# Loads and stores that ScalarE's queue may issue beside SyncE's, in a planned attention and FFN kernel on one Trainium2 core

## The chip, the core and the metric

The kernel runs on one core of one Trainium2 chip. A core has TensorE for matrix products (PE in the profile, with its weight loads on a row of their own, PEld), VectorE (DVE), ScalarE (ACT), GpSimd (POOL) and SyncE (SP), which here does nothing but issue transfers (DMAs). Each engine works through its instructions in the order of the program and starts one when the semaphores it waits for have been set. A transfer is issued on an engine's queue, which takes that engine some time, and is then carried out by the core's 16 DMA engines. The metric is the device time of one execution in microseconds (us).

## The reference

Causal attention over 8 batches, 8 heads, 576 positions and head size 64, with a bias from a cumulated sum, then a two-layer network with an ELU between its layers (4608 rows, 512 to 2048 to 512). All in float32:

```python
scores = scale * np.matmul(q, k.transpose(0, 1, 3, 2))          # scale = 1 / 8
cum = np.cumsum(np.maximum(s, 0.0), axis=-1)
bias = -(cum[:, :, :, None] - cum[:, :, None, :])
scores = np.where(causal, -1000000000.0, scores + np.minimum(bias, 0.0))
attn = softmax(scores)
x = rows_of(np.matmul(attn, v))                                 # 4608 x 512
h = x @ w_in
g = np.where(h > 0.0, h, np.exp(np.minimum(h, 0.0)) - 1.0)
return g @ w_out
```

## The kernel before

**Tiles and stages.** The attention works on pairs of heads, 32 of them (8 batches, 4 pairs). For each pair `prepare_pair` (L1018) loads the keys of both heads (`stk`) and the queries (`stq`; six transfers a pair at most), takes their largest values on ScalarE (the lines with `junk` as output, L699 and L702), scales and splits each into two 16-bit halves (`parts`), writes these to DRAM (`spread<-parts`) and reads them back in the layout of the products (`set<-spread`). `softmax_block` (L1130) computes for one block of 128 query rows the score products (`sc`, L1141), mask and row minimum on VectorE (`mn`, L1144) and the exponential on ScalarE (`p`, L1149). The first 64 rows of both heads are a small block of their own, with `None` at the end of its names (`tr_None`, `psh_None`). `halved` (L1170) writes the normalized rows as two 16-bit halves, and `turned_load` (L479) has a transposing DMA (`T<-p`, DMA_TRANSPOSE) turn them, 4 to 17 units of 128 x 128 at a time, because `weighing` (L1279) needs them turned for its products with the values (`av`, L1328). The values come by batch in `group_values` (L973, `va`), with their own largest values (L702) and halves (`v`). The attention's rows go to DRAM (`x_dram<-x`) and come back as columns (`xc<-x_dram`).

The network runs over 18 chunks of 256 rows, `moe_chunk` (L1457): first layer `h` (L1499, L1503: three products of 16-bit halves of x and w_in), ELU in steps on ScalarE and VectorE (`g` L1515, L1522 or L1526, `h` L1535, `gg` L1539 and L1542), second layer `o` (L1560), the output copy `ost` (L1586) and its store `out_dram<-ost` (L1612). Chunks and attention pairs are mixed so that TensorE has products of the one while the other is being prepared. The two weights are loaded (`raws`) and split at the start, until about 204 us.

**What sets the order.** No loop of the code is the order of the program. Every operation is recorded as an `Op` with its reads and writes and one or more *ways*: an engine, a cost in ns that the code assumes, the function that emits it, and for a transfer also its bytes and the time it is taken to be under way. `run` (L249) then places one operation after another: of all that may come next, the way that would be finished first on its engine, and of the operations the one that could start earliest; among those of that engine that could start as early, the one with the least deadline (`late`) goes first. `issue` (L234) makes eight trial runs; after each, `deadlines` (L211) goes back through the order and gives each operation the time by which it must start for the run to end as it did. The deadlines of the best trial give the order that is emitted. So a number such as `SP_COST` is no duration on the chip: it decides which order is built.

All 863 transfers of the program are issued by SyncE: `load` (L475) and `turned_load` offer only that way. SyncE's assumed cost is 500 ns for a load, 640 for those of keys and queries, and for a transposing DMA 170 ns a unit but at least 1330.

At the start TensorE gets *fillers* (L1618 to L1623: transposes of the identity into `scratch`, whose result nobody reads) wherever the plan has nothing else for it, until 60 us of the plan's time. They are ops too, and up to 300 of them may be placed.

## Time and profile before

| | us |
|---|---|
| median of 3 runs (lowest, highest) | 1020.22 (1017.01, 1020.98) |
| profiled execution, device time | 1021.47 |
| profiled execution, span | 1019.7 |
| mean granted clock of TensorE | 0.998 |

The span is the time from the first to the last instruction; the device time of the same execution is 1.8 us more. The busy tenths of the engines in 40 equal slices, with the share of the DMA engines:

```profile
PE   8999999999989999999999999999999999999998
DVE  6899899989989898999998998898979898744343
ACT  5999776776667676676776777666657665533232
DMA  7888743688999997899889999989979998521000
```

Each digit is a share in tenths, 9 standing for 90% or more. What an engine is called busy with leaves out the issuing of transfers. The same profile's chain, followed back from the last instruction, and its costliest groups of instructions (line, engine, operation, output<-inputs, count, busy us, mean ns of one, idle us just before them and what ended most of it):

```profile
PE h L1503 19%; PE o L1560 19%; PE sc L1141 3%; PE av L1328 3%; DMA T<-p 1%; DVE p L1209 1%; DVE p L1144 1%; DMA stq<-in_qT_dram 0%; DVE gg L1542 0%; DVE h L1535 0%; DMA spread<-parts 0%; ACT p L1149 0%; DVE p L1203 0%; DVE parts L1064 0%; ACT g L1522 0%
...
L1503 PE MATMUL h<-xh,wp 128*128 128x256 f16 x2176 | 401.5, 273 | 0.0
L1560 PE MATMUL o<-wp,gg 128*128 128x512 f16 x1632 | 391.2, 379 | 4.1 <-DVE tops L723 1.5
L1503 PEld LDWEIGHTS <-wp 128*128 128x128 f16 x3264 | 317.4, 98 | 66.1 <-issue 1.3
L1503 PE MATMUL h<-xl,wp 128*128 128x256 f16 x1088 | 296.9, 273 | 0.0
```

### The profile page before, as it was taken

Reading aid. Unit: us, or ns where it says so; the run is one execution under the profiler, and the core shown is the slowest. Engines: PE = TensorE matmul, PEld = TensorE weight load, DVE = VectorE, ACT = ScalarE, POOL = GpSimd, SP = SyncE. Lnnn points to the kernel's source line nnn. Section 1 sums busy time; section 2 is a strip of 40 time slices with the busy share of each in tenths; the row PEclk is TensorE's granted clock in tenths of the full one; section 3 lists DMA queues with packets and bytes.
Section 4 is the critical chain, followed back from the end, with each engine's and each line's share of the span. In section 5 each row is a group of like instructions: output and inputs, shape, how many; then the busy total and the mean of one; then the engine's idle time right before and its main releaser. Section 6 shows DMA issues by size and latency. Waiting matters only on the chain.

```text
span 1019.7 us, 21777 instructions
## 1 busy us (share of the span) xinstructions
PE 997.2 (98%) x7327; PEld 686.5 (67%) x7327; DVE 846.5 (83%) x2352; ACT 660.1 (65%) x1583; POOL 261.1 (26%) x429
## 2 busy tenths in 40 slices
PE   8999999999989999999999999999999999999998
PEld 7677666666656666666666666666766666666665
DVE  6899899989989898999998998898979898744343
ACT  5999776776667676676776777666657665533232
POOL 6332272423232323322222222221412330100000
PEclk9999999999999999999999999999999999999999
DMA  7888743688999997899889999989979998521000
GB/s 205 251 256 274 208 130 87 133 224 162 195 205 205 225 224 178 191 223 214 184 181 225 199 185 203 239 185 240 189 177 217 204 210 180 92 69 43 1 22 21
DMA packets 296724, 179.83 MB, mean 176 GB/s; under 512 B 209908, under 2 KB 270564, under 8 KB 296612
## 3 DMA queue, kind: packets, MB, share of 16 engines
q1 hardware_dynamic: 296612, 178.45, 76.6%
q8 instruction: 57, 0.93, 0.4%
q14 instruction: 55, 0.45, 0.1%
HBM read 93.08 MB, written 36.81 MB: 127 GB/s over the span
## 4 chain that ended last, share of the span: by engine, by line
PE 45%; DVE 4%; DMA 2%; issue 1%; ACT 1%; SPq 0%; DVEq 0%; ACTq 0%
PE h L1503 19%; PE o L1560 19%; PE sc L1141 3%; PE av L1328 3%; DMA T<-p 1%; DVE p L1209 1%; DVE p L1144 1%; DMA stq<-in_qT_dram 0%; DVE gg L1542 0%; DVE h L1535 0%; DMA spread<-parts 0%; ACT p L1149 0%; DVE p L1203 0%; DVE parts L1064 0%; ACT g L1522 0%
## 5 line engine op out<-in xcount | busy, mean ns | idle before, releaser
L1503 PE MATMUL h<-xh,wp 128*128 128x256 f16 x2176 | 401.5, 273 | 0.0
L1560 PE MATMUL o<-wp,gg 128*128 128x512 f16 x1632 | 391.2, 379 | 4.1 <-DVE tops L723 1.5
L1503 PEld LDWEIGHTS <-wp 128*128 128x128 f16 x3264 | 317.4, 98 | 66.1 <-issue 1.3
L1503 PE MATMUL h<-xl,wp 128*128 128x256 f16 x1088 | 296.9, 273 | 0.0
L1560 PEld LDWEIGHTS <-gg 128*128 128x128 f16 x1632 | 156.8, 98 | 152.8 <-DVE gg L1542 5.9
L1149 ACT ACTIVATE p<-p,mn 128x192 f32<-128x192 f32 (+1 forms) x232 | 144.0, 621 | 80.1 <-DVE mn L1144 77.5
L1209 DVE SCALAR_TENSOR_TENSOR p<-p,sm,p 128x512 f16<-128x512 f32 (+3 forms) x258 | 155.1, 630 | 3.4 <-ACT p L1205 1.5
L1515 ACT ACTIVATE g<-h,cs 128x512 f32<-128x512 f32 x136 | 92.4, 679 | 77.1 <-PE h L1503 75.5
L1539 ACT ACTIVATE gg<-h 128x512 f16<-128x512 f32 x127 | 75.4, 593 | 85.5 <-DVE h L1535 84.7
L1542 DVE SCALAR_TENSOR_TENSOR gg<-h,gg 128x512 f16<-128x512 f32 x136 | 93.2, 685 | 25.0 <-ACT gg L1539 24.5
L1141 PE MATMUL sc<-set 128*128 128x288 f16 (+3 forms) x544 | 109.7, 298 | 2.9 <-DVE mn L1144 1.6
L1144 DVE CUSTOM_DVE_ANT_0 p<-sc,maskw 128x192 f32<-128x192 f32 (+1 forms) x232 | 108.6, 480 | 4.2 <-PE sc L1141 1.8
L1535 DVE SCALAR_TENSOR_TENSOR h<-g,cs,h 128x512 f32<-128x512 f32 x136 | 101.9, 749 | 9.1 <-ACT g L1522 5.2
L1201 POOL TENSOR_SCALAR p<-p,sm 128x512 f16<-128x512 f32 (+3 forms) x78 | 53.6, 691 | 217.6 <-DVE sm L1155 80.3
L1205 ACT ACTIVATE p<-p,sm 128x512 f16<-128x512 f32 (+3 forms) x152 | 79.1, 532 | 26.5 <-ACT p L1149 8.3
L1526 DVE TENSOR_SCALAR g<-g 128x512 f32<-128x512 f32 x81 | 36.3, 448 | 58.1 <-ACT g L1515 57.7
L1141 PEld LDWEIGHTS <-set 128*128 128x128 f16 x584 | 55.1, 98 | 35.8 <-issue 6.0
L1328 PEld LDWEIGHTS <-v 128*64 128x64 f16 x960 | 48.5, 111 | 24.4 <-issue 13.7
L1328 PE MATMUL av<-T,v 128*64 128x256 f16 (+5 forms) x960 | 62.3, 281 | 2.1 <-DMA T<-p 2.0
L500 POOL TENSOR_SCALAR v<-va,scales 128x320 f16<-128x320 f32 (+1 forms) x41 | 25.3, 620 | 98.7 <-PE av L1328 66.8
L500 POOL TENSOR_SCALAR xh<-xc,cs 128x512 f16<-128x512 f32 x22 | 16.7, 760 | 130.0 <-PE h L1503 127.0
L1149 ACT ACTIVATION_READ_ACCUMULATOR p<-p,mn 128x1 f32 x232 | 43.6, 188 | 0.0
(205 smaller groups left out, 1271.2 us busy)
## 6 DMA issues: line engine op xcount, KB each, us to landing
set<-spread SPq DMA_DIRECT2D x32, 432.0 KB
spread<-parts_None SPq DMA_DIRECT2D x32, 288.0 KB
set<-spread SPq DMA_DIRECT2D x32, 288.0 KB
raws<-in_w_in_dram SPq DMA_DIRECT2D x16, 512.0 KB
raws<-in_w_out_dram SPq DMA_DIRECT2D x16, 512.0 KB
out_dram<-ost SPq DMA_DIRECT2D x32, 256.0 KB
va<-in_vb_dram SPq DMA_DIRECT2D x16, 352.0 KB
xc<-x_dram SPq DMA_DIRECT2D x22, 256.0 KB
```

Source lines behind the costliest of these rows:

```text
L1141: pe_.matmul(view(sc.v[:, :cw]), l, r, start=n == 0, stop=n == len(pairs) - 1)
L1144: op(prio, [("DVE", 168 + cw + 55 * (i > 0), lambda i=i, sc=sc: dve.tensor_tensor_reduce(pt.v[:, i * cw : (i + 1) * cw], sc.v[:, :cw], mv( ...
L1149: op(prio, [("ACT", 383 + w / 1.2, lambda: act.activation(pt.v[:, :w], pt.v[:, :w], AF.Exp, bias=mn.v[:, n - 1 : n], scale=-1.0, accum_out ...
L1205: ("ACT", 295 + size / 1.2, lambda part=part: act.activation(part(0), own(part), AF.Copy, scale=sm.v[:, r])),
L1209: ("DVE-SB", dve_2(size), lambda part=part: dve.scalar_tensor_tensor(part(1), own(part), sm.v[:, r], part(0), ALU.mult, ALU.subtract)),
L1328: pe_.matmul(av.v[w.h * HB : (w.h + 1) * HB, dst], w.values.v[:, w.h, kb, v], part(w, kb, m), start=kb == 0 and m == 0 and v == 0, stop=kb ...
L1503: pe_.matmul(columns(k), weight_part(f, 0, part)[1]()[:, c * P : (c + 1) * P], xx.v[:, c], start=(c == 0 and m == 0), stop=(c == NCB - 1 a ...
L1515: op(side, [("ACT", act_c(W) + (0 if native else 90), lambda: act.activation(g.v, hp.v, AF.Exp, scale=1.0 if native else by(3)))], [hp] + ...
L1535: op(side, [("DVE", dve_p(W) + 60, lambda: dve.scalar_tensor_tensor(hp.v, g.v, by(2 if sign[0] else 1), hp.v, ALU.mult, ALU.max))], [g, cs ...
L1539: ("ACT", act_c(W), lambda: act.activation(gg.v[:, 0], hp.v, AF.Copy, scale=2.0**-DOWN)),
L1542: op(side, [("DVE", dve_p(W), lambda: dve.scalar_tensor_tensor(gg.v[:, 1], hp.v, 2.0**-DOWN, gg.v[:, 0], ALU.mult, ALU.subtract))], [hp, ( ...
L1560: pe_.matmul(acc[i].v, gg.v[:, g, at], weight_part(f, 1, part)[1](), start=(f == 0 and m == 0), stop=(f == NF - 1 and m == 2),)
```

## The change

`load` can be given `either=True`; then the plan has two ways for that transfer, SyncE's queue and ScalarE's, with 600 ns assumed for an issue on ScalarE. This is set for the loads of values, keys and queries and for the stores of the result. The assumed costs of SyncE's own issues rise (500 to 520, 170 to 195 a unit, at least 1440 for a transposing DMA). In `deadlines` a filler no longer sets a deadline for what stands before it. The trial runs go from eight to six. The deadline by which the order is sorted is kept apart from the one being worked out (`due` and `late`).

```diff
--- before.py
+++ after.py
@@ -43,7 +43,8 @@
 
 N_CUT, CUT, N_LOW = 4, 2, 3
 PRIO_LOW = 10
-SP_COST, SP_SHORT, SP_TURN = 500.0, 640.0, 170.0
+SP_COST, SP_SHORT, SP_TURN = 520.0, 640.0, 195.0
+ACT_COST = 600.0
 
 N_FREE = 0
 
@@ -92,7 +93,7 @@
 
 
 class Op:
-    __slots__ = ("ways", "after", "before", "behind", "bufs", "new", "prio", "ready", "left", "filler", "late", "at", "frees")
+    __slots__ = ("ways", "after", "before", "behind", "bufs", "new", "prio", "ready", "left", "filler", "late", "at", "due")
 
 
 class Plan:
@@ -186,7 +187,7 @@
             d.before.append(o)
         for d in firsts:
             d.behind.append(o)
-        o.left, o.ready, o.late = len(o.after) + len(firsts), {}, 0.0
+        o.left, o.ready, o.due = len(o.after) + len(firsts), {}, 0.0
         self.ops.append(o)
         return o
 
@@ -215,21 +216,21 @@
             engine, start, stop, lag = o.at
             t = late.get(engine, end)
             for d in o.before:
-                if d.at is not None:
+                if d.at is not None and not d.filler:
                     t = min(t, d.late - lag - self.HOPS.get((engine, d.at[0]), self.HOP))
             for b in o.bufs:
                 for d in b.followed:
                     t = min(t, d.late - lag - self.HOPS.get((engine, d.at[0]), self.HOP))
             t -= stop - start
             for d in o.behind:
-                if d.at is not None:
+                if d.at is not None and not d.filler:
                     t = min(t, d.late)
             o.late = t
             if engine in late:
                 late[engine] = t
 
     ENDS = ("PE",)
-    ROUNDS, WAIT = 8, {"PE": 0.0, "DVE": 0.0, "ACT": 0.0, "Pool": 0.0, "SP": 0.0}
+    ROUNDS, WAIT = 6, {"PE": 0.0, "DVE": 0.0, "ACT": 0.0, "Pool": 0.0, "SP": 0.0}
 
     def issue(self):
         best = None
@@ -238,11 +239,13 @@
             self.wait = n > 0
             end, order = self.run(False)
             if best is None or end < best[0]:
-                best = end, self.wait, [(o, o.late) for o in self.ops]
+                best = end, self.wait, [(o, o.due) for o in self.ops]
             self.deadlines(order, end)
+            for o in order:
+                o.due = o.late
         _, self.wait, lates = best
-        for o, late in lates:
-            o.late = late
+        for o, due in lates:
+            o.due = due
         self.reset()
         return self.run(True)
 
@@ -317,7 +320,7 @@
             until, engine = first[0] + (self.WAIT[first[2]] if self.wait else 0.0), first[2]
             start, _, _, n, o = min(
                 (x for x in found if x[2] == engine and (x[0] <= until and not x[4].filler or x is first)),
-                key=lambda x: (x[4].late, x[1]))
+                key=lambda x: (x[4].due, x[1]))
             if o.filler:
                 start -= GAP
             engine, cost, trace = o.ways[n][:3]
@@ -472,13 +475,14 @@
     op = plan.op
     act, dve, pool, pe_ = nc.scalar, nc.vector, nc.gpsimd, nc.tensor
 
-    def load(prio, dst, src, reads, writes, nbytes, late=(), lag=LAG, cost=SP_COST):
-        return op(prio, [("SP", cost, lambda: nc.sync.dma_start(dst(), src()), lag, nbytes)],
-                  reads, writes, late)
+    def load(prio, dst, src, reads, writes, nbytes, late=(), lag=LAG, cost=SP_COST, either=False):
+        ways = [("SP", cost, lambda: nc.sync.dma_start(dst(), src()), lag, nbytes),
+                ("ACT", ACT_COST, lambda: act.dma_start(dst(), src()), lag, nbytes)]
+        return op(prio, ways[: 1 + either], reads, writes, late)
 
     def turned_load(prio, units, dst, src, reads, writes):
 
-        op(prio, [("SP", max(1330.0, SP_TURN * units), lambda: nc.sync.dma_start_transpose(dst(), src()), LAG,
+        op(prio, [("SP", max(1440.0, SP_TURN * units), lambda: nc.sync.dma_start_transpose(dst(), src()), LAG,
                    units * P * P * 2.2)], reads, writes)
 
     def rounded(prio, n, dst, src, reads, writes, sign=1.0, only=None):
@@ -981,10 +985,10 @@
         va = plan.buf(sb, [P, NP, nv, D], F32, f"va_{at}", tag=home.key[1])
         for j in range(NP):
             load(prio + j, lambda j=j: va.v[:, j, :whole], lambda j=j: vb[u.b, j, :, s0 : s0 + whole], [],
-                 [(va, (j, "whole"))], P * whole * D * 4)
+                 [(va, (j, "whole"))], P * whole * D * 4, either=True)
             for rows in HALF[: nv - whole]:
                 load(prio + j, lambda j=j, rows=rows: va.v[rows, j, whole:], lambda j=j: vb[u.b, j, :HB, s0 + whole : s0 + nv],
-                     [], [(va, (j, rows.start))], HB * 2 * D * 4)
+                     [], [(va, (j, rows.start))], HB * 2 * D * 4, either=True)
             peak(prio, nv * D, lambda j=j: va.v[:, j], values_of(va, j), first + j, mybir.AxisListType.XY,
                  aside=lambda: unread(nv * D).rearrange("p (n d) -> p n d", d=D))
         scales_of(prio, [(first, NP + 1)], col)
@@ -1026,15 +1030,15 @@
         spread = spreads[pair_sets.index(o)]
         for m, rows in enumerate(HALF):
             load(prio, lambda m=m, rows=rows: sk.v[rows, :n], lambda m=m: kT[b, :HB, 2 * j + m, :n], [], [(sk, m)],
-                 HB * n * 4, cost=SP_SHORT)
+                 HB * n * 4, cost=SP_SHORT, either=True)
         for m, rows in enumerate(HALF):
             if c0:
                 at = (1 - m) * (w - HB)
                 load(prio, lambda rows=rows, at=at: sq.v[rows, at : at + HB],
-                     lambda m=m: qT[b, j, :HB, m * HB : (m + 1) * HB], [], [(sq, (m, 0))], HB * HB * 4, cost=SP_SHORT)
+                     lambda m=m: qT[b, j, :HB, m * HB : (m + 1) * HB], [], [(sq, (m, 0))], HB * HB * 4, cost=SP_SHORT, either=True)
             load(prio, lambda m=m, rows=rows: sq.v[rows, m * c0 : m * c0 + nb * P].rearrange("d (i t) -> d i t", t=P),
                  lambda m=m: qT[b, j, :HB, P:].rearrange("d (i m t) -> d i m t", m=2, t=P)[
-                     :, u.blocks[0] : u.last + 1, m], [], [(sq, (m, 1))], HB * P * nb * 4, cost=SP_SHORT)
+                     :, u.blocks[0] : u.last + 1, m], [], [(sq, (m, 1))], HB * P * nb * 4, cost=SP_SHORT, either=True)
         peak(prio, w, lambda: sq.v[:, :w], [sq], 0, aside=lambda: unread(w), dst=pk)
         peak(prio, n, lambda: sk.v[:, :n], [sk], 1, aside=lambda: unread(n), dst=pk)
 
@@ -1611,7 +1615,7 @@
                     r0 = b * S + r + lo - t
                     load(side, lambda r0=r0, n=up - lo: out[r0 : r0 + n, :],
                          lambda ost=ost, o=slice(lo - i * P, up - i * P): ost.v[o],
-                         [ost], [], (up - lo) * DM * 4)
+                         [ost], [], (up - lo) * DM * 4, either=True)
                 t += n
         return following
```

In the program built after the change, 176 of the 863 transfers are on ScalarE: 54 of 72 loads of keys, 75 of 112 of queries, 26 of 44 of values and 21 of 40 stores. Since the order of all engines comes out of the plan, it is another one from the start. Three places, each with the rows of the program as it stands in the queue (line, operation, output<-input, shape, and xN for N such rows in sequence; the number at a name's end is the tile's own, and lines after the change are 1 to 4 higher).

SyncE before, at its start, from the loads of the first pairs to the first piece of the weights (`kl` are keys, `vs` and `va` values, `raws` weights):

```order
L476 DMA vs_115<-in_vb_dram 128x448
L476 DMA kl_2_122<-in_kT_dram 64x2x320
L476 DMA vs_133<-in_vb_dram 128x448
L476 DMA va_138<-in_vb_dram 128x320 x4
L476 DMA va_138<-in_vb_dram 64x128 x8
L476 DMA low_queries<-in_qT_dram 64x640
L476 DMA sums_dram<-aux 64x576
L476 DMA kl_1_109<-aux 1x2x320
L476 DMA kl_3_255<-in_kT_dram 64x2x320
L476 DMA raws<-in_w_in_dram 128x4x256
```

SyncE after, the same place:

```order
L479 DMA vs_121<-in_vb_dram 128x448
L479 DMA kl_2_131<-in_kT_dram 64x2x320
L479 DMA vs_141<-in_vb_dram 128x448
L479 DMA va_94<-in_vb_dram 64x128 x3
L479 DMA kl_3_232<-in_kT_dram 64x2x320
L479 DMA sums_dram<-aux 64x576
L479 DMA kl_1_114<-aux 1x2x320
L479 DMA low_queries<-in_qT_dram 64x640
L479 DMA raws<-in_w_in_dram 128x4x256
```

and ScalarE after, the first rows of its program:

```order
L685 ACT_TABLE_LOAD
L685 ACTIVATE junk<-ident 128x1
L480 DMA va_94<-in_vb_dram 128x320 x3
L480 DMA va_94<-in_vb_dram 64x128 x3
L480 DMA va_94<-in_vb_dram 128x320
L480 DMA va_94<-in_vb_dram 64x128 x2
L706 ACTIVATE junk,peaks<-va_94 128x448
```

Nine of the twelve loads of values have gone from SyncE's start to ScalarE's, ahead of ScalarE's first work on them; the first weights stand nine rows nearer to SyncE's start.

SyncE before, where pair 1's queries (`stq_1_None`) are loaded, some 280 us into the profiled execution:

```order
L476 DMA stq_1_None_3778<-in_qT_dram 64x64
L476 DMA stq_1_None_3778<-in_qT_dram 64x4x128
L476 DMA spread_1445<-parts_0_None_3755 256x1x576 x2
L476 DMA stq_1_None_3778<-in_qT_dram 64x4x128
L476 DMA stq_1_None_3778<-in_qT_dram 64x64
L476 DMA stk_2_None_3851<-in_kT_dram 64x576
L481 DMA_TRANSPOSE T_2_0_0_3854<-p_4_2_0_0_0_3813 128x4x128
L481 DMA_TRANSPOSE T_2_0_0_3854<-p_4_2_0_0_0_3813 128x6x128
```

SyncE after, the same queries:

```order
L479 DMA stq_1_None_3443<-in_qT_dram 64x4x128
L479 DMA stq_1_None_3443<-in_qT_dram 64x64
L479 DMA stq_1_None_3443<-in_qT_dram 64x4x128
L479 DMA spread_1499<-parts_0_None_3412 256x1x576 x2
L479 DMA xc_1_3497<-x_dram 128x2x256
L485 DMA_TRANSPOSE T_1_0_0_3524<-p_4_1_0_0_0_3507 128x4x128
```

and ScalarE after, from its one load of these queries to the work that reads them:

```order
L480 DMA stq_1_None_3443<-in_qT_dram 64x64
L1519 ACTIVATE g_1_3451<-h_1_3383,cs_2874 128x512
L1153 ACTIVATE p_161,sm_1_0_0_3356<-p_161,mn_1_0_0_2_3437 128x448
L1526 ACTIVATE g_1_3451<-g_1_3451 128x512
L1153 ACTIVATE p_168,sm_1_0_0_3356<-p_168,mn_1_0_0_3_3449 128x576
L480 DMA stk_2_None_3490<-in_kT_dram 64x576 x2
L1209 ACTIVATE p_4_1_0_0_0_3507<-p_125,sm_1_0_0_3356 128x2x128
```

One of the four loads has gone to ScalarE, between its other work, and both loads of the next pair's keys with it. The three that stayed now stand ahead of an earlier half of the pair's transposes (`T_1_0_0`); the four of `T_2_0_0` come 20 rows behind them.

SyncE before, around two transposes of 17 units, some 790 to 801 us into the execution:

```order
L481 DMA_TRANSPOSE T_1_0_2_11165<-p_2_1_0_2_2_11100 128x17x128
L476 DMA set_1902<-spread_1602 64x2x1152
L476 DMA set_1902<-spread_1602 64x1152
L476 DMA set_1902<-spread_1602 64x3456
L476 DMA set_1902<-aux_dram 3x2x576
L476 DMA xc_1_11244<-x_dram 128x2x256
L476 DMA out_dram<-ost_1_11032 128x512
L476 DMA stk_2_0_2_11257<-in_kT_dram 64x576
L476 DMA x_dram<-x_0_1_2_11251 128x256
L481 DMA_TRANSPOSE T_1_1_2_11282<-p_2_1_1_2_2_11200 128x17x128
```

SyncE after, around the same two:

```order
L485 DMA_TRANSPOSE T_1_0_2_11108<-p_2_1_0_2_2_11009 128x17x128
L479 DMA x_dram<-x_0_1_2_11115 128x256
L479 DMA set_1840<-spread_1654 64x2x1152
L479 DMA set_1840<-spread_1654 64x1152
L479 DMA set_1840<-spread_1654 64x3456
L479 DMA xc_0_11180<-x_dram 128x2x256
L485 DMA_TRANSPOSE T_1_1_2_11203<-p_2_1_1_2_2_11138 128x17x128
```

The store of the result and the keys that stood between the two transposes are no longer there; five issues lie between them where eight did.

## The prediction

> **What bounds the kernel now.** I read the page's head first, then the busy time by stage, then who waited for whom on TensorE and ScalarE, and last the timeline around the longest of those waits.
>
> ```profile
> span 1019.7 us, 21777 instructions
> PE 997.2 (98%) x7327; PEld 686.5 (67%) x7327; DVE 846.5 (83%) x2352; ACT 660.1 (65%) x1583; POOL 261.1 (26%) x429
> ```
>
> TensorE is busy 98% of the span and the change leaves its products alone, so only its gaps can be won: 1019.7 less 997.2 is 22.5 us. The stages say where they lie (stretch in us, its length, busy us of PE, PEld, DVE, ACT, POOL, then clock, share of the DMA engines, GB/s):
>
> ```profile
> 0.00:76.50 76.50, 71.02 (x494) 56.11 (x496) 64.19 (x215) 60.32 (x189) 34.51 (x91) 1.00 0.82 237
> 127.50:204.00 76.50, 74.27 (x501) 50.01 (x500) 74.93 (x194) 55.83 (x134) 37.23 (x46) 1.00 0.48 117
> 204.00:357.00 153.00, 145.58 (x1087) 97.58 (x1086) 136.82 (x394) 104.53 (x258) 45.98 (x69) 1.00 0.95 203
> 357.00:867.00 510.00, 506.63 (x3917) 347.71 (x3916) 456.86 (x1285) 347.35 (x808) 125.83 (x187) 1.00 0.93 202
> 867.00:1020.00 153.00, 148.71 (x1071) 100.14 (x1069) 68.92 (x128) 50.63 (x88) 5.82 (x10) 0.99 0.18 41
> ```
>
> 5.5 us of gap lie in the start, 2.2 in the stretch where the weights are split and VectorE is full (74.9 of 76.5), 4.3 at the end. Between 204 and 867 us, where nearly all the moved transfers are, the gaps are 7.4 + 3.4 = **10.8 us**. VectorE is at 593.7 of 663 there (90%), ScalarE at 451.9 (68%). TensorE's own waits in that stretch (us in total, times, longest):
>
> ```profile
> PE tr_None L1294 <- ACT psh_None L1166: 2.2, 1, 2.2
> PE av L1328 <- DMA T<-p: 2.0, 1, 2.0
> PE sc L1141 <- DVE mn L1144: 1.6, 3, 0.8
> PE sc L1141 <- DVE pc_None L1227: 1.1, 1, 1.1
> PE o L1560 <- DVE gg L1542: 1.0, 3, 0.5
> PE av_None L1287 <- ACT x_None L1340: 1.0, 1, 1.0
> PE o L1560 <- ACT gg L1539: 0.8, 1, 0.8
> ```
>
> The names at their ends are ScalarE and VectorE, but those had been waiting themselves. ScalarE's waits for loads in the same stretch:
>
> ```profile
> ACT junk L702 <- DMA stq_None<-in_qT_dram: 7.8, 6, 2.9
> ACT junk L702 <- DMA va<-in_vb_dram: 6.3, 6, 3.0
> ACT junk L702 <- DMA stq<-in_qT_dram: 5.2, 6, 1.8
> ```
>
> That is 19.3 us of ScalarE standing before a load of queries or values. The longest, on SyncE's queue:
>
> ```profile
> 283.02 2.51 SPq L476 DMA_DIRECT2D stq_None<-in_qT_dram  x2
> 285.57 0.60 SPq L476 DMA_DIRECT2D stk_None<-in_kT_dram  x1
> 286.27 6.10 SPq L481 DMA_TRANSPOSE T<-p  x4
> 292.42 0.65 SPq L476 DMA_DIRECT2D x_dram<-x_None  x1
> ```
>
> and on ScalarE and TensorE:
>
> ```profile
> 289.02 0.68 ACT L702 ACTIVATE junk<-stq_None 128x576 bf16<-128x576 f32 x1 [2.93 <-DMA stq_None<-in_qT_dram]
> 291.95 0.33 PE L1294 MATMUL tr_None<-ident,psh_None 128*128 128x128 f32 x1 [2.17 <-ACT psh_None L1166]
> ```
>
> SyncE issues without a break (9.86 of the 10.05 us from 283.02 to 293.07), the last query load goes out as late as 285.53, ScalarE stands until 289.02, and what is queued behind it there, the small block's softmax, lets TensorE stand 2.17 us. So **SyncE's issuing is a second full engine**, and the page shows it only through others' waits. The other large gap has the same root:
>
> ```profile
> 801.31 4.78 SPq L481 DMA_TRANSPOSE T<-p  x1
> 809.81 1.10 PE L1328 MATMUL av<-T,v 128*64 128x256 f16 x9 [2.02 <-DMA T<-p]
> ```
>
> **The change part by part.** The sum is made against the profiled execution: span 1019.7, device time 1021.47. The median shown, 1020.22, is 1.25 us less.
>
> 1. *Issues that leave SyncE.* 176 of 863 are ScalarE's now: 54 of keys, 75 of queries, 26 of values, 21 stores. SyncE's prices (ns, least/median/most):
>
> ```profile
> L476 SPq DMA_DIRECT2D stk_None<-in_kT_dram x40: 466/594/1136, 77.8 to 503.3; - x40
> L476 SPq DMA_DIRECT2D stq_None<-in_qT_dram x80: 466/618/1514, 79.7 to 530.0; - x80
> L476 SPq DMA_DIRECT2D va<-in_vb_dram x44: 328/430/596, 6.7 to 787.7; - x44
> L476 SPq DMA_DIRECT2D out_dram<-ost x40: 332/513/1692, 144.4 to 1016.8; - x40
> L481 SPq DMA_TRANSPOSE T<-p x168: 1205/1326/5427, 160.9 to 895.9; - x168
> ```
>
> 54 x 0.594 + 75 x 0.618 + 26 x 0.430 + 21 x 0.513 = 100.5 us leave SyncE. At the place of the first gap the three query loads left on SyncE now stand 20 rows ahead of the transposes they stood directly before; at the second, five issues instead of eight lie between two transposes. I take away those of TensorE's waits whose chain runs through such a transfer: tr_None 2.2, av 2.0, av_None 1.0 (behind a query load too), one of the three waits on mn, 0.8, and the one on ScalarE's gg, 0.8. The last two by these rows, of the chain that ended last and of ScalarE:
>
> ```profile
> 616.25 4.56 DMA stq<-in_qT_dram
> ```
>
> ```profile
> 349.35 0.79 ACT L702 ACTIVATE junk<-va 128x704 bf16<-128x704 f32 x1 [2.95 <-DMA va<-in_vb_dram]
> ```
>
> Sum **-6.8 us**. At most all 10.8 go; at least none, if the order leaves others as late. I take 6.8 because each piece has its row.
>
> 2. *What ScalarE gets.* No row of before shows it issuing. One issue costs it between 0.33 (the least of va) and 1.51 us (the most of stq_None); I take SyncE's medians, 0.57 on average. Some 148 of the 176 lie between 204 and 867 us: +84. Counted by line, the new order also takes about 23 us of work from ScalarE, some 18 of it there. 451.9 + 84 - 18 = 518 of 663, 78%, still under VectorE's 90%: **0 us**, covered by ScalarE's idle time. Behind an issue stand exponentials and the gg copies, and TensorE waits for those; without the cover it is the third rival.
>
> 3. *What moves to VectorE.* 13 of the L1526 steps go from ScalarE (L1522) to it:
>
> ```profile
> L1526 DVE TENSOR_SCALAR g<-g 128x512 f32<-128x512 f32 x81 | 36.3, 448 | 58.1 <-ACT g L1515 57.7
> L1522 ACT ACTIVATE g<-g 128x512 f32<-128x512 f32 x63 | 39.5, 627 | 1.3
> ```
>
> 13 x 0.448 = 5.8 us, and 4.4 more from the other lines: +10.2. Its idle time between 204 and 867 falls from 69 to 59 us. What stays of TensorE's waits on VectorE (0.8 + 1.1 + 1.0) grows in that ratio: **+0.5**, between 0 and 3.
>
> 4. *The start.* The order places 26 more filler products, 164 for 138.
>
> ```profile
> 12.87 3.88 PE L1623 MATMUL scratch<-ident 128*128 128x128 f32 x34
> ```
>
> ```profile
> 6.75 6.86 SPq L476 DMA_DIRECT2D va<-in_vb_dram  x12
> ```
>
> At 0.114 us each they cost 3.0 us if TensorE had work, nothing if it would have stood anyway, which is what they are placed for. Against that, 9 of the 12 value loads (6.86 us) go out beside SyncE's queue, where the first weights stand behind them. -2 to +3, I take **0**, since TensorE has 5.5 us of gaps there beside the fillers.
>
> 5. *The counted prices, the deadlines without fillers, six rounds for eight*: no instruction of their own; all they do is the order, counted above. The last four stores stay on SyncE: the end costs **0**.
>
> Sum: -6.8 + 0.5 = -6.3, so 1015.2 for an execution like the profiled one and 1013.9 for the median: **1014**.
>
> **The rivals.** *Nothing is won.* The transfers are late in the DMA engines, not in the queue: their share is 0.95 and 0.93 in the stage rows, and the query load above took from 285.53 to 289.0 after its issue had ended. A moved load then lands as late as before, and the 0.5 of VectorE and up to 3 us of fillers stay: 1020 to 1023; I put it at 1020. Against it: two stretches where issuing itself took 2.5 and 4.8 us. The Trainium skill, page "DMA: Bandwidth & Descriptors", section "Issuing engines are not separate DMA queues", says that DMAs started by different engines end up on the same 16 engines, and that starting from several saves only the time of issuing. By that rule the part of the waits that is landing stays, and the sum would lose most of its 6.8 us; the DMA shares agree with it, the long issues speak against it.
>
> *ScalarE becomes the bound* (the slower side). Its queue runs in order, so an issue that is held holds the exponentials behind it. In the built program each DMA counts its landing on one of eight counters, taken in turn over both queues, and waits until the DMA eight before has landed. On one queue that costs next to nothing:
>
> ```profile
> SPq L476 <- DMA set<-spread: 2.8, 4, 1.1
> ```
>
> On two, eight issues pass in less time, and the wait may fall on ScalarE. Its room up to VectorE's 594 us is 594 - 434 = 160 us, over 148 issues: it decides from **1.08 us per issue**, held time included. Price: the stretch with a full VectorE has TensorE idle 2.9%, which over 663 us is 19.3 for 10.8, +8.5; if 357 to 867 became like 204 to 357 (4.8% idle), +21. I take 12, nearer to the row with a full engine: 1032. The Trainium skill, page "Perfetto Trace Analysis", section "DMA Instruction — HWDGE (DVE, Sync)", says that the block that makes the descriptors is shared by the issuing sequencers and locked by one at a time. By that rule an issue on ScalarE would also wait for a transpose on SyncE, up to its 5.4 us; no run here shows two queues yet.
>
> **How the numbers follow.** About 0.5% is what a measurement of this kernel tells from no change, 5.1 us: faster is below 1015.1, slower above 1025.3. Forecast 0.47, its own range 1007 (all 10.8 us and the 2 of the start gone) to 1017; a little of it, 0.06, is within 0.5%. Nothing won 0.27. ScalarE bound 0.26, nearly all of it slower. So faster 0.41, same 0.34, slower 0.25. The range runs from 1007 into the third case, 1030, leaving out its upper half (0.13) and a little below.
>
> **What would show it.** Right: ScalarE's waits for stq, stq_None and va shrink from 19.3 us to under 7, SyncE shows pauses between issues, PE's gaps between 204 and 867 us fall to about 4, ScalarE's issues last about 0.6 us. Wrong: those issues last over 1.1 us or ScalarE stands before them; waits of PE on ScalarE's p and gg in place of those removed; gaps of PE in the first 77 us grown by more than 3 us.

## The result, and the profile after

The changed kernel takes **1052.99 us** (median of 6 runs, 1049.78 to 1059.03) against 1021.52 (6 runs): 1.0318 times as long, 95% interval 1.0283 to 1.0354. The profiled execution took 1057.83 us. One run of e3 below took 1147.53 us at a granted clock of 0.851, where its others took 1035 to 1038, and is left out of e3's time. The changed kernel's head in the profile, and the stages between which the prediction divided the gaps (columns as before):

```profile
span 1056.0 us, 21830 instructions
...
PE 1010.1 (96%) x7353; PEld 694.9 (66%) x7353; DVE 856.0 (81%) x2375; ACT 644.3 (61%) x1551; POOL 271.6 (26%) x439
```

```profile
0.00:76.50 76.50, 66.94 (x476) 53.74 (x477) 59.92 (x195) 56.90 (x174) 31.59 (x85) 0.98 0.77 228
204.00:357.00 153.00, 147.00 (x1108) 100.02 (x1106) 137.84 (x407) 101.20 (x252) 46.41 (x68) 1.00 1.03 207
357.00:867.00 510.00, 487.44 (x3683) 331.82 (x3684) 443.82 (x1251) 324.58 (x765) 129.84 (x190) 0.98 0.94 192
```

TensorE's gaps have grown from 22.5 to 45.9 us, and its busy time from 997.2 to 1010.1. 357 to 867 us, the best stretch before (3.4 us of gap), now has 22.6; the start has 9.6 for 5.5. The clock, 1.00 in these three rows before, is 0.98 in two of them. TensorE's waits over the span, the four largest:

```profile
PE av L1332 <- DMA T<-p: 15.0, 4, 6.0
PE o L1564 <- ACT gg L1543: 7.0, 5, 2.7
PE sc L1145 <- DVE mn L1148: 6.9, 12, 1.6
PE trl L922 <- DVE pl L1168: 3.8, 1, 3.8
```

and ScalarE's waits that a transfer ended (rows of the same view for that engine):

```profile
ACT g L1519 <- DMA set<-spread: 4.4, 1, 4.4
ACT p L1153 <- DMA set<-spread: 4.0, 1, 4.0
...
ACT junk L706 <- DMA stq_None<-in_qT_dram: 2.7, 3, 1.2
ACT gg L1543 <- DMA x_dram<-x_None: 2.5, 1, 2.5
...
ACT junk L706 <- DMA stq<-in_qT_dram: 0.8, 1, 0.8
```

ScalarE hardly stands before its own loads any more (junk: 3.5 us where the prediction's three rows had 19.3). In their place stand g, p and gg, which read nothing of `set` or `x_dram`: the engine was standing at one of the new issues ahead of them. Counted in the trace behind the first 30 us, TensorE's waits longer than 0.5 us come to 31.4 us: 15.0 are the waits on T, and ten others, 11.7 us together, began no more than 5 us after such a stand had ended, all five on `gg` among them. The longest stall, on SyncE, TensorE and ScalarE:

```profile
726.36 4.45 SPq L485 DMA_TRANSPOSE T<-p  x1
730.91 0.53 SPq L479 DMA_DIRECT2D va<-in_vb_dram  x1
731.55 8.98 SPq L485 DMA_TRANSPOSE T<-p  x1
```

```profile
739.44 0.85 PE L1332 MATMUL av<-T,v 128*64 128x256 f16 x6 [5.98 <-DMA T<-p]
```

```profile
744.79 3.85 ACTq L480 DMA_DIRECT2D stk<-in_kT_dram  x2
748.75 0.67 ACT L1153 ACTIVATE p<-p,mn 128x448 f32<-128x448 f32 x1 [4.01 <-DMA set<-spread]
```

One transpose's issue lasted 8.98 us (5.43 was the longest before), and TensorE stood for its data. Behind it, two issues of keys took ScalarE 3.85 us from the first to the end of the second, and the exponential behind them started when a `set` load had landed. How fast the packets went, in 8 us of this stall and in 2 us just behind it (queue, packets, MB, share of 16 engines; q1 is SyncE's queue, q10 ScalarE's):

```profile
q1 hardware_dynamic: 1930, 0.50, 90.9%
q10 hardware_dynamic: 151, 0.33, 30.3%
```

```profile
q1 hardware_dynamic: 1732, 0.45, 123.0%
q10 hardware_dynamic: 47, 0.02, 4.0%
```

The first pair is 729 to 737 us, the second 740 to 742. Three value loads (packets of 2560 bytes) were in q10 from 726.4 to 738.5 us. Beside them SyncE's queue moved 241 packets a microsecond; behind them 866. Taken over all stretches of 2 us between 204 and 867 us with 50 or more of its 256-byte packets, the median is 216 a microsecond in the 16 with eight or more of the 2560-byte packets in q10, and 432 in the 127 with nothing in q10, a tenth of which are above 804; so the 866 is near the best of this queue. The other two long waits on T, at 662 and 812 us, fall into the other two groups of such loads (655 to 665 and 804 to 815).

### The profile page after: what moved, and what is told of

The parts are those of the page before. It is cut to its first block, busy times and chain, and to the rows that moved or that the text cites. A ratio compares the mean times of both kernels' runs of the same rounds, so it can differ in the third digit from the quotient of the medians.

```text
span 1056.0 us, 21830 instructions
## 1 busy us (share of the span) xinstructions
PE 1010.1 (96%) x7353; PEld 694.9 (66%) x7353; DVE 856.0 (81%) x2375; ACT 644.3 (61%) x1551; POOL 271.6 (26%) x439
## 5 line engine op out<-in xcount | busy, mean ns | idle before, releaser
L1564 PE MATMUL o<-wp,gg 128*128 128x512 f16 x1632 | 395.9, 383 | 8.7 <-ACT gg L1543 7.0
L1145 PE MATMUL sc<-set 128*128 128x288 f16 (+3 forms) x544 | 112.7, 299 | 5.6 <-DVE mn L1148 5.4
L1205 POOL TENSOR_SCALAR p<-p,sm 128x512 f16<-128x512 f32 (+3 forms) x84 | 60.6, 725 | 217.7 <-DVE sm L1159 90.5
L1546 DVE SCALAR_TENSOR_TENSOR gg<-h,gg 128x512 f16<-128x512 f32 x136 | 93.2, 685 | 26.4 <-ACT gg L1543 25.5
L1539 DVE SCALAR_TENSOR_TENSOR h<-g,cs,h 128x512 f32<-128x512 f32 x136 | 102.0, 750 | 10.8 <-ACT g L1526 6.7
L1530 DVE TENSOR_SCALAR g<-g 128x512 f32<-128x512 f32 x94 | 41.8, 445 | 67.3 <-ACT g L1519 66.8
L1209 ACT ACTIVATE p<-p,sm 128x64 f16<-128x64 f32 (+3 forms) x140 | 72.8, 530 | 28.7 <-DMA T<-p 11.6
L1145 PEld LDWEIGHTS <-set 128*128 128x128 f16 x584 | 55.3, 98 | 42.0 <-issue 10.8
L1332 PE MATMUL av<-T,v 128*64 128x256 f16 (+5 forms) x960 | 66.2, 288 | 15.2 <-DMA T<-p 15.0
L1332 PEld LDWEIGHTS <-v 128*64 128x64 f16 x960 | 51.8, 114 | 36.1 <-issue 26.3
L504 POOL TENSOR_SCALAR v<-va,scales 128x320 f16<-128x320 f32 (+1 forms) x41 | 29.3, 716 | 72.3 <-PE av L1332 54.9
```

The source lines that it names most:

```text
L1145: pe_.matmul(view(sc.v[:, :cw]), l, r, start=n == 0, stop=n == len(pairs) - 1)
L1209: ("ACT", 295 + size / 1.2, lambda part=part: act.activation(part(0), own(part), AF.Copy, scale=sm.v[:, r])),
L1332: pe_.matmul(av.v[w.h * HB : (w.h + 1) * HB, dst], w.values.v[:, w.h, kb, v], part(w, kb, m), start=kb == 0 and m == 0 and v == 0, stop=kb ...
L1539: op(side, [("DVE", dve_p(W) + 60, lambda: dve.scalar_tensor_tensor(hp.v, g.v, by(2 if sign[0] else 1), hp.v, ALU.mult, ALU.max))], [g, cs ...
L1546: op(side, [("DVE", dve_p(W), lambda: dve.scalar_tensor_tensor(gg.v[:, 1], hp.v, 2.0**-DOWN, gg.v[:, 0], ALU.mult, ALU.subtract))], [hp, ( ...
L1564: pe_.matmul(acc[i].v, gg.v[:, g, at], weight_part(f, 1, part)[1](), start=(f == 0 and m == 0), stop=(f == NF - 1 and m == 2),)
```

## The experiments

Times are medians; ratios are against the kernel before on the same chip, which took 1021.5 to 1022.7 us on the chips used. An interval reaches 2 to 7 us to each side, so a difference of less than some 4 us between two rows is not clear of noise. "Held" is ScalarE's idle time directly before one of its issues, added up over waits longer than 0.3 us: "landing" where the counter of the transfer eight before was what came last (within 0.1 us of the start), "other" where an engine was. Where both came close together the division is good to 3 us; the sums are not touched by it.

| kernel | issues on ScalarE | held by landing, other, us | time | ratio (95%) |
|---|---|---|---|---|
| the change | 176 | 26.1, 14.1 | 1052.99 | 1.0318 (1.0283 to 1.0354) |
| e1 prices and order alone | 0 | 0 | 1014.89 | 0.9931 (0.9903 to 0.9959) |
| e2 change, late values on SyncE | 159 | 26.8, 10.3 | 1033.58 | 1.0116 (1.0084 to 1.0149) |
| e3 change, all but the first nine on SyncE | 9 | 6.1, 0 | 1035.69 | 1.0140 (1.0106 to 1.0174) |
| e4 change, only values on ScalarE | 26 | 11.3, 2.1 | 1042.61 | 1.0204 (1.0173 to 1.0234) |
| e5 planned anew, values never | 155 | 15.7, 12.3 | 1038.22 | 1.0145 (1.0112 to 1.0177) |
| e6 e1's plan, late values on ScalarE | 32 | 11.1, 1.4 | 1025.93 | 1.0034 (1.0011 to 1.0057) |
| e7 e1's plan, keys and queries on ScalarE | 184 | 2.0, 5.3 | 1018.01 | 0.9949 (0.9931 to 0.9967) |
| e8 choice for the first values alone | 9 | 6.0, 0 | 1020.53 | 0.9979 (0.9955 to 1.0002) |
| e9 e1 with the second trial's plan | 0 | 0 | 1018.29 | 0.9975 (0.9950 to 0.9999) |
| e10 change with the third trial's plan | 176 | 34.5, 7.6 | 1048.72 | 1.0273 (1.0218 to 1.0329) |
| e11 e5 with ACT_COST 60 | 208 | 20.8, 9.2 | 1093.65 | 1.0713 (1.0646 to 1.0779) |
| e13 e1's plan, all late ones on ScalarE | 256 | 19.8, 5.9 | 1030.42 | 1.0086 (1.0056 to 1.0115) |
| e14 e5 with the rule of 2 us | 51 | 0.3, 8.0 | 1022.66 | 1.0001 (0.9980 to 1.0022) |
| e14b e5 with the rule of 4 us | 28 | 0, 2.3 | 1020.78 | 0.9992 (0.9972 to 1.0012) |
| e16 choice for keys alone | 63 | 19.4, 4.1 | 1028.18 | 1.0055 (1.0033 to 1.0077) |
| e17 e6 with each load in halves | 64 | 22.6, 1.4 | 1051.42 | 1.0291 (1.0246 to 1.0335) |

**e1: the order without the second queue.**

```diff
-        return op(prio, ways[: 1 + either], reads, writes, late)
+        return op(prio, ways[:1], reads, writes, late)
```

> All transfers stay on SyncE; the new costs, the deadlines without fillers and the six trial runs stay. Theory M (two queues mix in the DMA engines: the value loads' packets of 2560 bytes on ScalarE's queue slow the transposing DMAs of SyncE's queue, and TensorE waits for T<-p): no second queue, so 1016 to 1027, av's wait on T<-p under 3 us against 15.0. Rival O (it is the new order and its prices, whoever issues): 1040 or more, with T<-p waits like those of the change. Rival A (ScalarE's queue: its exponentials stand behind issues of any kind): 1016 to 1027, as by M.

Measured 1014.89, 1.1 us under the lowest range given: what is not the second queue makes the kernel a little faster. The same program is built, row by row, when only the three prices are changed, and the one of before when only the prices are set back: of these edits the prices are all that counts. TensorE's gaps between 204 and 867 us are 663 less these two:

```profile
204.00:357.00 153.00, 151.06 (x1132) 102.52 (x1130) 138.01 (x415) 109.65 (x264) 44.09 (x70) 1.00 0.92 206
357.00:867.00 510.00, 507.49 (x3929) 348.19 (x3927) 452.64 (x1267) 353.36 (x817) 115.60 (x171) 1.00 0.94 203
```

4.5 us for 10.8 before, with all 863 transfers on SyncE.

**e2, e3, e4: the change's plan, other queues.** TensorE's, VectorE's and GpSimd's rows stay as they are; a transfer that the plan gave to ScalarE is issued by SyncE at its place. The line of e2 is shown; each call of `load` names its `kind`, e3 sends every kind but the first values to SyncE, and e4 keys, queries and stores:

```diff
-                ("ACT", ACT_COST, lambda: act.dma_start(dst(), src()), lag, nbytes)]
+                ("ACT", ACT_COST, lambda: (nc.sync if kind == "values" else act).dma_start(dst(), src()), lag, nbytes)]
```

> The plan of the change, row by row, on TensorE, VectorE and GpSimd; only the 17 loads of values behind the first nine are issued by SyncE at the place the plan gave them, the 159 others stay on ScalarE. M: the waits of av on T<-p (15.0 us, of which 13.8 in three places near 662, 733 and 812 us) fall under 4, and the clock lost behind them comes back: 1053 less 11 to 20, 1033 to 1042, and the transposes of 17 units stay under 6 us of issue (8.98 before). O: 1050 to 1056, the waits at the same places. A: 17 of 176 issues gone, 1050 to 1054.

> The plan of the change again; 167 of the 176 are issued by SyncE at the plan's place, the first nine value loads stay on ScalarE. M: no mixing behind the start, so 1028 to 1042, with the 3.8 us at the start left and SyncE as full as before; O: 1050 or more; A: 1024 to 1032, well under the kernel with the late values alone on SyncE.

> The plan of the change; keys, queries and stores (150 of the 176) are issued by SyncE, the 26 value loads stay on ScalarE. M: the transposes are slowed as in the change, av waits for T<-p 10 us or more, 1046 to 1058. O: 1050 to 1056. A: 26 of 176 issues left on ScalarE, 1024 to 1034.

e2 and e3 came out as the mixing of two queues would have it; rival A, issues of any kind on ScalarE, missed e2, e3 and e4. Moving 17 loads of 176 gives 19.4 us back, and the waits on transposes go (second line of this kernel's waits; 15.0 in the change):

```profile
PE o L1564 <- ACT gg L1543: 4.2, 3, 1.8
PE av L1332 <- DMA T<-p: 2.8, 2, 1.5
```

ScalarE was held nearly as long as in the change (37.1 us for 40.2), so this part is the transposes and the clock lost behind them (granted 0.998 for 0.985). e4 missed: the time came 3.4 us under its range and av waited 2.9 us for T, not 10 or more. The late values alone on ScalarE met the transposes less: by the count of 2 us stretches above they were under way together for 4 us there and for 32 in the change. The waits on T are long only where the two met for long: e13 has 14 us together and 2.1 waited, e6 20 and 2.7, e10 24 and 8.8, the change 32 and 15.0.

e3 sets a limit to the other half of the account. It takes 150 more issues off ScalarE than e2, and 31 us of holds with them, and is no faster (1035.69 for 1033.58). SyncE then has these issues again, at places chosen for two queues. So in the change's own plan the price of the holds can't be told from that of the plan.

**e5, e7, e9, e10: the plan or the queue?** The edit of e5 is shown, for the first of its two loads of values; the others are as the table says.

```diff
-                 [(va, (j, "whole"))], P * whole * D * 4, either=True)
+                 [(va, (j, "whole"))], P * whole * D * 4)
```

> Planned anew with the choice taken from all loads of values; keys, queries and stores keep it (155 issues on ScalarE by the plan). If the values were the whole loss (mixing in the engines behind, nine issues ahead of the first exponentials at the start): 1008 to 1017, the 1014.9 of the order alone or a little less. If transfers on ScalarE's queue cost by themselves, or the plan made for two queues is the worse one: 1022 to 1034, as the 1033.6 with the late values on SyncE says less the start's 2 to 5.

> The same plan; all 184 loads of keys and queries are issued by ScalarE at their places, 184 x 0.55 = 101 us of issuing. If ScalarE's queue is the cost (exponentials and gg behind issues that are held until a buffer is free): 1022 to 1045, with waits of TensorE on ScalarE's gg and on mn. If the plan was the cost of the change and not the queue: 1005 to 1016, since SyncE has 112 us less to issue.

> All transfers on SyncE and the new prices, but the plan of the second trial run (ROUNDS = 2), which is the trial that the change's own plan and that of the run without values come from; the order alone took the third. It has the 26 more fillers and more work on VectorE than the order alone. If which trial is taken is what costs (fillers and the order they bring): 1025 to 1036, near the 1038 without values. If it is the second queue in the plan (issues priced at 600 ns on ScalarE push its work to VectorE): 1013 to 1021.

> The change, all choices kept, with the plan of its third trial run instead of the second: 8 us less work on VectorE by the plan's costs and 18 fillers fewer, values, keys, queries and stores on both queues as in the change. If the trial or VectorE's work is the larger part: 1028 to 1042. If the queue's mixing and the start are: 1045 to 1056.

e5 is the surprise: without a single value load on ScalarE still 1038, above both ranges. e7, with more issues than the change but in the plan for one queue, loses 3.1 us against e1, hardly clear of noise; it lies between the two ranges, nearer to the plan's (2.0 above it, 4.0 below the queue's). So neither ScalarE's issuing time (184 issues, 111 us) nor the presence of a second queue is dear, and nothing is won by SyncE's 184 fewer issues. e9 and e10 rule out the choice of the trial run as the larger part: its fillers and order cost 3.4 us without the second queue, and the third trial saves the change 4.3, outside the range for it; both are within the noise. e5 and e7 differ in the "held" column, 28.0 against 7.3 us, but also in their whole plan. In e5's profile TensorE has 10.9 us more of gaps than in e1's, and its waits that follow a hold, counted as in the change, are 6.0 us. So the holds are seen in a part of e5's loss, not in all of it.

**e6, e13, e17: values under e1's plan.**

> The plan of the order alone (1014.9), row by row; its 32 loads of values behind the first twelve are issued by ScalarE at their places. Mixing (packets of two queues in the same engines slow the transposing DMAs): 1020 to 1034, transposes of 17 units with issues over 6 us (4.8 at most in the order alone) and waits of TensorE on T<-p over 3 us. If ScalarE's queue is what counts: 32 x 0.4 us of issues in its idle time, 1013 to 1018. If only the order counts: 1013 to 1017.

> The plan of the order alone (1014.9) row by row; keys, queries, stores and all values but the first twelve are issued by ScalarE, some 256 issues. If the costs of the parts add up (keys and queries 3.1, late values 11.0): 1027 to 1032. If value loads cost more where other loads share ScalarE's queue, as 19.4 in the change against 5.9 alone there: 1034 to 1050.

> The plan of the order alone with its 32 later value loads on ScalarE (1025.9 as they were), each issued as two halves, so that the packets have 1280 bytes in place of 2560. If large packets beside the transposing DMA's packets of 256 bytes are what slows it: 1015 to 1021. If sharing the engines at all is: 1022 to 1029. If issues held on ScalarE by the landing of the eighth transfer before are: 1025 to 1035, since there are twice as many issues.

e6 costs 11.0 us. ScalarE's longest stand in it, on SyncE and ScalarE:

```profile
709.19 4.36 SPq L485 DMA_TRANSPOSE T<-p  x1
713.59 0.46 SPq L479 DMA_DIRECT2D set<-aux_dram  x1
714.15 7.58 SPq L479 DMA_DIRECT2D spread<-parts  x4
```

```profile
722.16 0.34 ACTq L479 DMA_DIRECT2D va<-in_vb_dram  x1
722.54 0.69 ACT L1519 ACTIVATE g<-h,cs 128x512 f32<-128x512 f32 x1 [7.72 <-DMA set<-aux_dram]
```

The value load was held until the small `set` load of 713.59 had landed, which was issued behind a transpose of 4.36 us, and the first ELU step stood 7.72 us; TensorE then stood 2.1 us for `gg`. Its waits on T were under the 3 us expected (2.7), and no issue of a transpose over 6 us (5.1), so here the holding counts for more. e13's parts add up (1030.42 in 1027 to 1032). e17 was missed by all three: halves of 1280 bytes cost 25.5 us more than whole loads, with twice the issues and twice the time held by landings. Smaller packets cured nothing here; since the holds doubled with them, the run says no more of packet size.

**e8: the start.**

> Planned anew, the choice only for the first batch's loads of values: nine go to ScalarE at the start, everything else stays on SyncE. If the nine issues ahead of the first exponentials delay the start: 1018 to 1021, the first exponential at about 15 us where the order alone has 12 to 13, TensorE's first wait over 2 us. If the start is not it: 1013 to 1017.

5.6 us over e1. The first row is this kernel's longest wait on TensorE; the others are its ScalarE at the start:

```profile
PE trl L922 <- DVE pl L1168: 8.0, 1, 8.0
```

```profile
7.42 5.98 ACTq L480 DMA_DIRECT2D va<-in_vb_dram  x9
18.40 0.58 ACT L706 ACTIVATE junk<-va 128x448 bf16<-128x448 f32 x1 [16.17 <-DMA raws<-in_w_in_dram]
...
20.38 0.39 ACT L1153 ACTIVATE pl<-pl,mn 128x128 f32<-128x128 f32 x1
```

ScalarE is at the nine issues until 13.40 us, stands until 18.40 for a transfer, and starts the first softmax's exponential at 20.38; in e1 that row starts at 10.65. The time is in the range for a delayed start, but the delay is longer than the 15 us expected and than the change's own: there the issues end at 13.5 us, the exponential starts at 14.98, and TensorE's first wait is 3.8 us, not 8.0. So e8 does not price the change's start.

**e11: issues almost free in the plan.** ACT_COST 60 in e5.

> As the run without values (1038), with ACT_COST 60 in place of 600, so that the plan takes next to nothing from ScalarE for an issue: some 200 issues on ScalarE and about 13 us less work on VectorE by the plan's costs. If work pushed to VectorE was the cost: 1014 to 1024. If any plan with two queues costs: 1030 or more. If issues that are held on ScalarE's queue are the cost: above 1038, since there are 50 more.

1093.65. Both "any plan with two queues" and held issues had allowed for it, and it is far beyond e5, though with 30 us the issues are held as long as there. What differs is bunching: in the built program 129 of the 208 issues stand in blocks of three or more with no work of ScalarE's between them, 30 of 155 in e5, 13 of 184 in e7. A block of four is some 2.4 us in front of whatever is next, by an estimate from their mean of 0.61 us.

**e14, e14b, e16: a plan that knows the counters.** `landed` holds the landings that the plan expects; ScalarE's way may not start before the eighth last plus LANE (2 or 4 us):

```diff
+                                       landed[-8] + LANE if len(w) > 3 and w[0] == "ACT" else 0.0))
...
+                landed.append(end + lag)
```

> As the run without values (1038), but the plan may give a transfer to ScalarE only 2 us after the transfer eight before it has landed by the plan; 51 issues remain there. If issues held on ScalarE's queue (15.7 us of its standing before an issue ended by the eighth transfer's landing, 11.8 by VectorE) are the loss of the plan with two queues: 1014 to 1024, ScalarE's time held before issues under 8 us (30 without the rule). If a plan with two queues costs otherwise: the loss goes with the number of issues or more, 1024 to 1032.

> The same with 4 us: 28 issues on ScalarE. Held issues: 1012 to 1020, time held under 4 us. Otherwise: 1018 to 1026.

> The control for the rule: the choice for keys alone, 63 issues on ScalarE, 12 more than under the rule of 2 us, and nothing in the plan that keeps them from being held. Held issues: 1020 to 1030, with 8 us or more of ScalarE's time held. If only the number of issues counts: the same as the run under the rule, within 4 us.

The rule takes 15.6 us from e5, with a third of the issues. With 51 it is 5.5 us under the control with 63, 1.5 more than "within 4 us"; the two have nearly the same number of issues, and 8.3 us held against 23.5. But e5 is 10.0 us over the control with only 4.5 us more held, so the number of issues, or the plan that goes with it, costs too; e14's time held, 8.3 us, was a little over the 8 expected, but landings are 0.3 of it. e16 shows the place of the price again, on ScalarE and then on TensorE:

```profile
ACT p L1153 <- DMA x_dram<-x: 7.5, 1, 7.5
```

```profile
PE sc L1145 <- DVE mn L1148: 12.4, 11, 6.2
```

e14b, fully within its range of 1018 to 1026 for a cost by number, is 0.8 above that for held issues. No run with a second queue beats e1, which has the lowest median of all and beats both kernels.

## Why the prediction was wrong

**Step 2 failed**, "0 us, covered by ScalarE's idle time". Its terms were near: 176 issues of 0.572 us on average (0.57 taken), 15.8 us less work on ScalarE (about 23 taken), and step 3's VectorE at 856.0 (846.5 + 10.2 = 856.7). Wrong was to weigh them as a sum against ScalarE's room. Between 204 and 867 us its work, issues and holds come to some 535 of 663 us, and with all 40.2 us of standing an issue costs 0.80 us, under the 1.08 from which the third rival was to decide. ScalarE did not become full, and yet its waits reached TensorE: a single hold of up to 4.8 us stands in front of an exponential or an ELU step however idle the engine is on average, and 11.7 us of TensorE's waits followed such holds. The mechanism was the one named in that rival, the landing of the transfer eight before: 19 of ScalarE's 33 holds over 0.3 us. e14 against its control e16 is the test of it by the plan, 5.5 us for 15 us of holds. The rival's price, 1032, was 21 too low. The counters hold SyncE too: in the change 54 of its issues, for 67.5 us together, started as the transfer eight before landed (some of these landings were data that they needed anyway); before the change it was 4.6 us. What this costs no run separates.

**What no case had** is the transposes: 15.0 us of TensorE's waits, gone in e2 with 19.4 us of time. The Trainium skill's sentence on the same 16 DMA engines (page "DMA: Bandwidth & Descriptors", section "Issuing engines are not separate DMA queues"), told in the prediction, was used only for loads that land no earlier; that SyncE's transposes would be slowed by ScalarE's loads was not thought of.

**Step 1** forecast that waits for loads go, and they went (19.3 to 3.5 us). But its reading, SyncE as "a second full engine" whose issues bound the kernel, fell: between 204 and 867 us SyncE was issuing for 585 of 663 us before and for 474 in e7. e7 takes 184 issues off SyncE (111 us of ScalarE's time in their place) and gains nothing, e1 leaves all of it and has the 6.3 us of gaps back that the step had put at 6.8. So those gaps went with the order of the issues, not with their number.

**Step 4**, the start: 0 was taken, and what could stand behind the issues on ScalarE was not asked. TensorE's gaps there grew by 4.1 us (9.6 for 5.5), where the range had ended at +3; against e1, which has 7.5, it is 2.0. **Step 5** gave the prices no term of their own; e1 makes them -7.7. **Step 3** held for VectorE's work; TensorE's waits on mn grew to 6.9 us; that ScalarE's exponentials, which come between, are the cause was seen for three of them (0.8 to 1.6 us, each behind a hold) and is not shown for the rest.

By medians: e1 1014.9; e2 18.7 above it; the late values 19.4 on top; 1053. The 19.4 is shown by an edit of 17 issues. The 18.7 is not divided: the start, the holds and a plan made for two queues are all in it, and e3, with hardly a hold, is as slow. Such sums don't carry over: the late values cost 19.4 us in the change, 11.0 in e1's plan (e6) and 6.9 from e3 to e4. **Open** is also how the late values' cost divides in other plans (slow transposes in the change, holds in e6 and e17), and what part of e11's 79 us over e1 is bunching: that was counted, not tried by itself.

The Trainium skill's rule in the prediction (page "Perfetto Trace Analysis", section "DMA Instruction — HWDGE (DVE, Sync)"), a block for descriptors locked by one sequencer, would have ScalarE wait for SyncE's transposes. The trace disagrees: while a transpose was being issued from 731.55 for 8.98 us, ScalarE issued a load of queries at 739.58 in 0.62 us. Of its 176 issues 31 lie wholly within a transpose's issue; they took 0.56 us on average and 1.24 at most, the others 0.57 and 1.70.

## What to carry to other kernels

Before moving transfers to a computing engine's queue, ask what stands behind each issue and what can hold it, transfer by transfer; the engine's average idle time says nothing of that. Transfers that share counters over two queues tie the queues together, so a planner must know the counter, not only the issue's price. And a queue that is busy issuing for most of the time isn't yet a bound: try the same order with its work taken away, and another order with the work left.

## What the runs showed of the hardware

SyncE's queue, with its transposes, was slower beside value loads of ScalarE's: a median of 216 packets of 256 bytes a microsecond for 432 with ScalarE's queue empty, counted in the change as above. Other plans show the same (e10 260 for 436, e6 262 for 426, e13 338 for 459); what differs is for how long the two met. The Trainium skill, page "DMA: Bandwidth & Descriptors", section "Queues, rings and completion order", says that each DMA engine takes turns between the queues that have work, a packet at a time. The trace agrees in so far as both queues moved on together; in the 8 us of the stall it has 1930 packets of SyncE's to 151 of ScalarE's, so what the profile counts as packets did not alternate one for one.

A stall of TensorE costs more than its length (the change; columns as in the stages):

```profile
736.00:738.00 2.00, 0.00 (x0) 0.00 (x0) 0.00 (x0) 0.00 (x0) 0.00 (x0) 0.66 1.31 123
738.00:740.00 2.00, 0.56 (x6) 0.56 (x7) 0.00 (x0) 0.50 (x1) 0.42 (x1) 0.50 0.99 193
740.00:742.00 2.00, 2.00 (x25) 1.96 (x20) 1.70 (x3) 1.88 (x5) 0.56 (x2) 0.50 1.27 235
742.00:744.00 2.00, 2.00 (x8) 0.78 (x7) 1.91 (x4) 1.28 (x4) 0.00 (x0) 0.63 0.81 226
```

TensorE stood from 733.46 to 739.44; the granted clock fell to one half within the stall and stayed there until about 743.5 (0.63 over 742 to 744), some 4 us of work at half speed. The Trainium skill, page "TensorE: Matmul & The Clock Gate", Part 1, gives half the clock after an idle window of some 3.4 us, which agrees with this stall. A shorter one did it too, TensorE's wait of 2.72 us on `gg` from 355.63 to 358.35:

```profile
356.00:358.00 2.00, 0.00 (x0) 0.00 (x0) 1.97 (x4) 0.30 (x1) 0.00 (x0) 0.94 0.97 167
358.00:360.00 2.00, 1.65 (x5) 0.56 (x6) 2.00 (x7) 1.97 (x6) 0.00 (x0) 0.50 0.92 221
```

So a wait need not last 3.4 us to cost clock; here a hold on ScalarE of 3.7 us stood ahead of it. Over the execution the clock is 0.985 for 0.998: an estimate by these two is 1.3% of 1056, 14 us, of the 36 lost in the profiled execution. That is somewhat too much, since TensorE's busy time grew by 12.9 us in all, 1.9 of it for 26 more fillers; some 11 us by this second estimate. The other 23.4 us are gaps.
